# A linear-attention and feed-forward kernel on one core: the fifth token group's first dense product as seven block products, three copies of a round on ScalarE, attention steps 17 to 21 in one stretch

## The chip, the cores and the metric

The kernel runs on one core of one Trainium2 chip. The metric is the device time of the whole program in microseconds (us), lower is better. The engines are named as the profile names them: PE (TensorE, matrix multiply; PEld is its weight load), DVE (VectorE), ACT (ScalarE), POOL (GpSimd) and SP (SyncE, which issues the transfers here). Each engine works through its own list of instructions in order, and the engines wait for each other by semaphores.

## The reference

The program is a decayed linear attention followed by a feed-forward layer with a tanh GELU. Cut to what matters:

```python
# attention: q, k, v are (4, 8, 768, 64), blocks of 64 positions
for b in range(nb):
    intra = (qb @ kb^T * Dmask) @ vb
    inter = (qb * lam_pow) @ kv_state
    out[b] = intra + inter
    kv_state = lam_block * kv_state + (kb * rev_pow)^T @ vb
# feed-forward: x is (3072, 512), w_in (512, 2048), w_out (2048, 512)
h = x @ w_in                       # the first dense product
g = gelu_tanh(h)
return g @ w_out                   # the second dense product
```

## The kernel before

**Steps and token groups.** The attention is cut into 24 steps. A step is a batch's block of 256 tokens (SB) for one half of the heads, so that steps 2i and 2i+1 make token block i, of which there are 12. A step needs the loads of q, k and v (`load_step`), their scaling (`prep`: `cast_q` on DVE, `cast_k` on ACT, `scale_v` on POOL), a transposition by transfer (`transpose_dma`, issued by SP), the scores S on PE (`scores`), the causal mask on DVE that makes PT from S (`causal`), the products O = PT·v plus q·u and K = k·v on PE, the copy of O into xT on ACT (`x_out`), and the state: `update` makes t on DVE and u from t on POOL. `R(n, s)` does the scores and K of step n and the output of step s, one after the other; `burst(ns, ss)` does the same for several steps at once, with all scores first; `U(n)` is the second half of the state update of step n. The output O of a step needs u of that step and of the step two before it.

**Dense work as filler.** The 12 token blocks form seven groups, `groups` at L533: the fifth (g = 4) is blocks 6 and 7, so 512 tokens, the output of steps 12 to 15; g = 5 is steps 16 to 19, g = 6 is steps 20 to 23. As soon as a group's last x is out, `queue_group(g)` puts its dense work as small pieces into the list `filler`, and `fill(n)` runs the next n pieces. So the dense products lie on PE between the parts of the attention, in an order written by hand: the main program is a list of `burst`, `R`, `U`, `prep` and `fill` calls. `pin` keeps everything in the order of the program on each engine.

**First dense product, plain.** `mm1` (L556): for each of 16 strips of 128 columns of w_in four matmuls of 128x512 add up one PSUM bank, and one ACT instruction (L565) takes the GELU of it into gT. For a group of 512 tokens that is 64 matmuls.

**First dense product, seven block products.** Groups in `SEVEN` (L531: g = 5 and 6) use `seven(m, k)` (L726) instead. F, C and T halve w_in's columns, the contraction and the tokens. Seven products of blocks (and of sums of blocks) replace eight: `I_SUMS` are sums of blocks of w_in, made once by `sum_win`, `X_SUMS` sums of blocks of x, made for each group by `sum_x`. The work is cut into four rounds k = 0 to 3 of 256 columns of each half F. In a round each of the seven products is a piece of four matmuls of 128x256, in the order m = 1, 2, (4 of the round before), 5, 6, 3, 7. Products 1, 6, 7 and 4 add up in one bank X, of which there are two, one for even and one for odd rounds; 2 goes to a bank W; 5 and 3 add up in a bank Y. Between them the partial sums are taken out: after 1 the copy "m1" (ACT, L750), after 2 W is added to it (DVE, L760), after 5 the copy "q" (ACT), after 6 the copy "u2" (DVE, L752), after 3 Y is added to u2 (DVE), after 7 X is added to q (DVE). Because 7 adds into the same bank, it cannot start until u2 has been read out; in the same way 6 waits for the copy m1 and 3 for the copy q.

**Where the GELUs go.** The GELU of each of the four results (L756) isn't issued at once. It is put into the list `pending`, and `release()`, called right after the copy q of product 5, issues all that are pending. So in rounds 1 to 3 ACT's order is: copy q, then four GELUs (three of the round before and that of m1 of this round). In round 0 there is only one. After the last round they are issued as their sums are ready.

**Merging.** `merge` (L773) lays the pieces of `seven` between the remaining pieces of the group before (its second dense product, `product`, cut into halves of four matmuls). `SLOTS` says after which m such an old piece is put: under key 4 one old piece each after 2, 6, 3 and 7, so product 7 is the fifth piece after product 5; under key 5 there is one more after 5, so product 7 is the sixth.

**Second dense product.** `product` (L616) also uses seven block products. Its blocks of w_out and their sums are read, its own copies (L657) are on ACT.

**Order around the change before.** g = 4 is queued by `R(17, 15)`, with step 17 already under way; its first dense product is plain. Then come steps 18 and 19 in one burst, 20 and 21 in another with 32 plain matmuls of 128x512 between, and g = 5 is queued by the second with `lead` 11 and `per_set` 4.

Of the kernel before, what the change touches and what calls it, by code (L numbers as in the profile page):

```python
# [8 lines left out]
FP32 = mybir.dt.float32  # L9
FP16 = mybir.dt.float16  # L10
AF = mybir.ActivationFunctionType
ALU = mybir.AluOpType
# [3 lines left out]
def kernel(  # L16
# [10 lines left out]
    nc = tc.nc  # L27
    pin = tc.keep_in_program_order
    P = 128
    B, H, S, D = q.shape  # L30
    SB = 256
    NSB = S // SB
    HH = H // 2
    DM = H * D
    DFF = moe_w_in.shape[1]
# [9 lines left out]
    ld = ctx.enter_context(tc.tile_pool(name="ld", bufs=4))  # L45
    a16p = ctx.enter_context(tc.tile_pool(name="a16", bufs=5))
    qkp = ctx.enter_context(tc.tile_pool(name="qkp", bufs=5))
    ptp = ctx.enter_context(tc.tile_pool(name="ptp", bufs=3))
    ucp = ctx.enter_context(tc.tile_pool(name="ucp", bufs=3))
    ubp = ctx.enter_context(tc.tile_pool(name="ubp", bufs=4))  # L50
    xtp = ctx.enter_context(tc.tile_pool(name="xtp", bufs=3))
    gtp = ctx.enter_context(tc.tile_pool(name="gtp", bufs=2))
    mtp = ctx.enter_context(tc.tile_pool(name="mtp", bufs=1))
# [6 lines left out]
    def load_step(s, names="qkv"):  # L60
        b, r = divmod(s, 2 * NSB)
        sb, half = divmod(r, 2)
        ts = ld32.setdefault(s, [])
        for nm, src in (("q", q), ("k", k), ("v", v)):
            if nm not in names:
                continue
            t = ld.tile([P, HH, 2, D], FP32, tag=nm + "32", name=f"{nm}32_{s}")
            rows = src[b, half * HH : (half + 1) * HH, sb * SB : (sb + 1) * SB, :]
            queue = nc.scalar if (nm, s) == ("v", 0) else nc.sync
            pin(queue.dma_start(out=t[:].rearrange("p h j d -> p h (j d)"),  # L70
                                in_=rows.rearrange("h (p j) d -> p h (j d)", j=2)))
            ts.append(t)

    w_in16 = w16p.tile([P, NC, DFF], FP16)
    w_out16 = w16p.tile([P, NF, DM], FP16)


    HF, HE = NF // 2, DM // 2
# [65 lines left out]
    def sum_win(m, j, eng):  # L144

        if not wi_sum:
            wi_sum.extend(wst.tile([P, 2, 2, DFF // 2], FP16, tag=f"w{2 + i}", name=f"ws{i}")
                          for i in range(2))
        a, op, b = I_SUMS[m]
        cs, fs = slice(0, 2), slice(512 * j, 512 * j + 512)  # L150
        pin(eng.tensor_tensor(w_in_block(m, cs, fs), w_in_block(a, cs, fs),
                              w_in_block(b, cs, fs), op))
# [92 lines left out]
    def prep(s):  # L245
        prep_qk(s)
        prep_v(s)
# [8 lines left out]
    def prep_v(s):  # L256
        scale_v(s)
        if s >= 6:
            if s + 3 == FIRST_DMA_T + 2:
                load_step(s + 3, "qk")  # L260
            else:
                load_ahead(s + 3)
# [6 lines left out]
    def prep_qk(s):  # L269
        cast_qk(s)  # L270
        transpose_dma(s)

    def cast_qk(s):
        cast_q(s)
        cast_k(s)
# [252 lines left out]
                                for i in range(2)]  # L528
        return gs_kept[1:]

    SEVEN = (5, 6)  # L531
    SLOTS = {5: {1: 0, 2: 1, 5: 1, 6: 1, 3: 1, 7: 1}, 4: {1: 0, 2: 1, 5: 0, 6: 1, 3: 1, 7: 1}}
    groups = [[0, 1], [2], [3], [4, 5], [6, 7], [8, 9], [10, 11]]  # L533
    group_of = {sb: (g, i) for g, sbs in enumerate(groups) for i, sb in enumerate(sbs)}
# [9 lines left out]
    def queue_group(g, lead=0, per_set=0):  # L544
        N = len(groups[g]) * SB
        NTAU = N // P
        gT = gtp.tile([P, HF, 2, N], FP16, tag="gT", name=f"gT_{g}")
# [172 lines left out]
        of_set, pending = {}, []  # L720

        def release():
            while pending:
                pending.pop(0)()

        def seven(m, k):  # L726

            st = of_set.setdefault(k, {})
            for name in {1: "X", 2: "W", 5: "Y"}.get(m, ""):
                key = name + str(k % 2) if name == "X" else name  # L730
                if key not in hbank:
                    hbank[key] = ps_M.tile([P, 2, SB], FP32, tag="M", name="H" + name)
                st[name] = hbank[key]
            dst = st[{2: "W", 5: "Y", 3: "Y"}.get(m, "X")]
            a, b = X_FACTORS[m]
            for i in range(2):
                f = 2 * k + i
                for c in range(2):
                    pin(nc.tensor.matmul(  # L739
                        dst[:, i, :],  # L740
                        w_in_block(a, slice(c, c + 1), slice(f * P, f * P + P))[:, 0],
                        x_block(b, slice(c, c + 1))[:, 0],
                        start=(m in (1, 2, 5) and c == 0 and i == 0), stop=(m in (2, 3, 4) and c == 1),
                        skip_group_check=True))

            def copied(name, tag, eng):
                t = ld.tile([P, HH, 2, D], FP32, tag=tag, name=f"{name}_{g}_{k}")
                t = t[:].rearrange("p h j d -> p (h j d)").rearrange("p (i t) -> p i t", i=2)
                if eng is nc.scalar:
                    pin(nc.scalar.activation(out=t, in_=dst[:], func=AF.Copy))  # L750
                else:
                    pin(eng.tensor_copy(out=t, in_=dst[:]))  # L752
                st[name] = t

            def gelu(F, T, src):
                pin(nc.scalar.activation(out=gT[:, 2 * k : 2 * k + 2, F, T * SB : T * SB + SB],  # L756
                                         in_=src, func=AF.Gelu_apprx_tanh))

            def added(F, T, name):
                pin(nc.vector.tensor_tensor(st[name], dst[:], st[name], ALU.add))  # L760
                pending.append(lambda src=st[name]: gelu(F, T, src))

            if m == 1:
                copied("m1", "q32", nc.scalar)
            elif m == 2:
                added(0, 0, "m1")
            elif m == 5:
                copied("q", "q32", nc.scalar)
                release()
            elif m == 6:  # L770
                copied("u2", "k32", nc.vector)
            elif m == 3:
                added(0, 1, "u2")  # L773
            elif m == 7:
                added(1, 1, "q")
            elif m == 4:
                pending.insert(0, lambda: gelu(1, 0, dst[:]))
            if k == HF // 2 - 1 and m in (3, 7, 4):
                release()

# [72 lines left out]
        def behind(k, i0, i1, ms):  # L853

            piece = filler[at + k]

            def both():
                piece()
                sum_g(i0, i1, ms)

            filler[at + k] = both

        at = len(filler)
        order = [(m, p) for m in (1, 2, 5, 6, 3, 7, 4) for p in range(HN // P)]
        if g in SEVEN:
            merge(lead, per_set)
            parts = (0, 1) if g + 1 in SEVEN else (None,)
            for m, p in order:
                for part in parts:
                    filler.append(lambda m=m, p=p, part=part: product(m, p, part))  # L870
            at = len(filler) - len(order) * len(parts)
            for k, m in enumerate((2, 4, 3)):
                behind(len(parts) * k, 4, 8, (m,))
            return
        for i in range(HF):
            for fs in ([[i, i + HF]] if per == 2 else [[i], [i + HF]]):
# [1 line left out]
        for m, p in order:  # L878
            for part in (0, 1) if g + 1 in SEVEN else (None,):
                filler.append(lambda m=m, p=p, part=part: product(m, p, part))  # L880
# [9 lines left out]
        else:  # L890
            behind(9, 0, 4, (1, 2) if g == 3 else (1, 2, 4, 3))
            if g == 3:
                behind(12, 0, 4, (4, 3))
            w = 2 if g + 1 in SEVEN else 1
            for k, m in zip((0, 3, 7, 11) if w == 2 else (0, 1, 2, 4), (1, 2, 4, 3)):
                behind(n1 + k, 4, 8, (m,))

    def fill(n):
        for _ in range(min(n, len(filler))):
            filler.pop(0)()  # L900

    def R(n, s, ahead=None, keep=False):

        if n is not None:
            scores(n)
        if ahead:
            ahead()
        products(n, s)
        if n is not None:
            causal(n)  # L910
        if s is not None and s % 2 == 1:
            g, i = group_of[s // 2]
            if i == len(groups[g]) - 1 and g > 0:
                queue_group(g)
        if n is not None and not keep:
            update(n, 0)

    def U(n):
        update(n, 1)
# [138 lines left out]
            sum_win((n - 7) // 2, (n - 1) % 2, nc.vector)  # L1058

    cast_qk(16)  # L1060
    load_step(17, "qk")
    transpose_dma(16)
    load_step(17, "v")
# [13 lines left out]
    fill(1)  # L1077
    U(15)
    U(16)
    fill(8)  # L1080
    prep(18)
    R(17, 15)
    fill(1)
    U(17)
    fill(1)
    sum_win(3, 0, nc.vector)
    fill(2)
    prep(19)
    sum_win(3, 1, nc.vector)
    fill(2)  # L1090
    sum_win(4, 0, nc.vector)
    fill(2)
    sum_win(4, 1, nc.vector)
    fill(2)
    prep_qk(20)
    fill(1)
    prep_qk(21)
    prep_v(20)
    fill(3)

    burst((18, 19), (16, 17))
    prep_v(21)
    fill(2)
    U(18)
    U(19)
    fill(4)
    prep_qk(22)
    fill(2)
    burst((20, 21), (18, 19), 11, 4)
    fill(3)  # L1110
    U(20)
    U(21)
    fill(20)
    prep_qk(23)
    fill(23)
    prep_v(22)
    prep_v(23)
    fill(13)
    burst((22, 23), (20, 21))
    U(22)  # L1120
    U(23)
# [31 lines left out]
```

## Time and profile before

The time is the median of 3 runs; the profile is one execution of the program.

| | us |
|---|---|
| time, median of 3 runs | 199.15 |
| time, lowest and highest run | 198.92 and 199.36 |
| span of the profiled execution, first to last instruction | 197.1 |
| PE busy | 191.5 |
| DVE busy | 151.6 |
| ACT busy | 122.2 |
| POOL busy | 73.3 |
| from the page: share of the chain that ended last that lies on PE | 89% |

The profile names groups of instructions by line, engine, operation and tile, with the busy time of all of them, the mean duration of one and what ended the idle time before. A duration of one is longer than the distance between two of them: a matmul of 128x256 is listed with 273 ns, while 16 of them follow each other in 1.75 us in the chain. The timeline gives starts in us from the span's start, and the windows view gives for a stretch its length, the busy time of each engine, and the granted PE clock (1.00 is full).

### The profile page before, as it was taken

The page shows a single profiled execution, that of the slowest core. Times are in us where ns is not written, and L with a number is a line of the kernel's source. Part 1 is how long each engine was busy: PE and PEld are TensorE (multiplying, and loading weights), DVE is VectorE, ACT ScalarE, POOL GpSimd, SP SyncE. Part 2 cuts the span into 40 slices and gives each one's busy share as a digit, 9 for nine tenths or more (in the row PEclk, how much of TensorE's full clock was granted, in tenths as well). Part 3 has the DMA queues.
Part 4 walks back from the last instruction along what each step waited for, and adds up shares of the span by engine and source line. Part 5 has one row for each costly group of instructions (what it writes and reads, how often), then busy time and mean ns, then how long its engine had stood idle before and what let it go on. Part 6 is the DMA issues. An engine that isn't in the chain of part 4 may idle for free.

```text
span 197.1 us, 5915 instructions
## 1 busy us (share of the span) xinstructions
PE 191.5 (97%) x2431; PEld 140.0 (71%) x2431; DVE 151.6 (77%) x297; ACT 122.2 (62%) x249; POOL 73.3 (37%) x85
## 2 busy tenths in 40 slices
PE   8979999999999999999999999999999999999993
PEld 2556544446888888654688764588888888888882
DVE  4797622789999889849999937998668996588620
ACT  3673878357874685686835378844768845779221
POOL 6594123456554841068854517165002030002000
PEclk9999999999999999999999999999999999999999
DMA  6999999999999999999997998400220300030205
GB/s 172 290 324 384 387 387 388 299 287 292 236 216 225 259 343 220 213 266 247 271 268 149 268 328 213 88 4 0 53 85 25 109 6 0 0 110 0 106 19 197
DMA packets 62810, 38.13 MB, mean 193 GB/s; under 512 B 18624, under 2 KB 55744, under 8 KB 62784
## 3 DMA queue, kind: packets, MB, share of 16 engines
q1 hardware_dynamic: 62240, 37.50, 75.0%
q8 instruction: 19, 0.31, 0.6%
q10 hardware_dynamic: 544, 0.26, 0.5%
q14 instruction: 7, 0.06, 0.1%
HBM read 27.26 MB, written 6.29 MB: 170 GB/s over the span
## 4 chain that ended last, share of the span: by engine, by line
PE 89%; SPq 4%; DMA 4%; ACT 0%; issue 0%
PE Hps L561 25%; PE MX L640 18%; PE MY L640 9%; PE HX L739 7%; PE O2ps L576 7%; PE MW L640 4%; DMA wi<-in_moe_w_in_dram 4%; SPq L70 4%; PE HY L739 4%; PE S L350 3%; PE Hps L830 3%; PE HW L739 2%; PE OK L408 2%; PE O L461 1%; PE O L436 1%; PE OK L399 1%
## 5 line engine op out<-in xcount | busy, mean ns | idle before, releaser
L561 PE MATMUL Hps<-xT,w_in 128*128 128x512 f16 (+1 forms) x288 | 50.5, 332 | 0.0
L513 POOL TENSOR_TENSOR u<-t,lumask 128x256 f16<-128x256 f32 x40 | 30.9, 787 | 39.5 <-DVE t L506 25.8
L561 PEld LDWEIGHTS <-w_in 128*128 128x128 f16 x288 | 27.9, 98 | 19.1
L565 ACT ACTIVATE gT<-Hps 128x512 f16<-128x512 f32 x56 | 33.3, 597 | 11.3 <-PE Hps L561 10.8
L360 DVE TENSOR_TENSOR PT<-S,mask 128x512 f16<-128x512 f32 x48 | 30.3, 681 | 7.5 <-PE S L350 7.5
L266 POOL TENSOR_TENSOR v<-v,dv 128x512 f16<-128x512 f32 x24 | 27.7, 1156 | 18.2 <-DMA v<-in_v_dram 14.2
L640 PEld LDWEIGHTS <-gs 128*128 128x128 f16 x320 | 31.2, 98 | 3.6
L640 PEld LDWEIGHTS <-gT 128*128 128x128 f16 x240 | 23.3, 98 | 3.2 <-ACT gT L565 0.2
L640 PE MATMUL MX<-w_sum,gs 128*128 128x256 f16 x160 | 21.4, 273 | 0.0
L282 DVE TENSOR_TENSOR qk<-q,dq 128x512 f16<-128x512 f32 x23 | 18.4, 802 | 1.7 <-DMA q<-in_q_dram 1.7
L692 POOL TENSOR_TENSOR o<-u,q 128x512 f32<-128x512 f32 (+1 forms) x5 | 6.3, 1253 | 35.2 <-ACT u L657 35.2
L295 ACT ACTIVATE qk<-k 128x512 f16<-128x512 f32 x23 | 14.4, 625 | 7.4 <-DMA k<-in_k_dram 7.2
L610 DVE TENSOR_TENSOR gs<-gT 128x1024 f16<-128x1024 f16 (+1 forms) x24 | 16.9, 711 | 1.6 <-ACT gT L565 1.6
L576 PE MATMUL O2ps<-w_out,gT 128*128 128x512 f16 x64 | 14.6, 379 | 0.0
L487 ACT ACTIVATE xT<-OK 128x256 f16<-128x256 f32 x26 | 9.9, 452 | 6.7 <-PE OK L408 6.2
L739 PEld LDWEIGHTS <-ws 128*128 128x128 f16 x128 | 12.5, 97 | 1.8
L657 ACT ACTIVATE u<-MX 128x256 f32<-128x256 f32 x18 | 6.9, 384 | 10.1 <-PE MX L640 10.1
L487 ACT ACTIVATE xT<-O 128x256 f16<-128x256 f32 x22 | 8.0, 459 | 5.3 <-PE O L461 4.5
L576 PEld LDWEIGHTS <-gT 128*128 128x128 f16 x64 | 6.1, 98 | 6.6
L640 PE MATMUL MY<-w_out,gs 128*128 128x256 f16 x80 | 10.7, 273 | 0.0
L350 PEld LDWEIGHTS <-qkT 64*64 64x64 f16 x384 | 6.0, 106 | 6.6 <-issue 3.6
L640 PE MATMUL MX<-w_sum,gT 128*128 128x256 f16 x80 | 10.4, 273 | 0.0
(96 smaller groups left out, 317.3 us busy)
## 6 DMA issues: line engine op xcount, KB each, us to landing
q<-in_q_dram SPq DMA_DIRECT2D x24, 256.0 KB, 5.1
k<-in_k_dram SPq DMA_DIRECT2D x24, 256.0 KB, 5.1
v<-in_v_dram SPq DMA_DIRECT2D x23, 256.0 KB, 5.4
out_dram<-o SPq DMA_DIRECT2D x23, 256.0 KB, 4.2
wo<-in_moe_w_out_dram SPq DMA_DIRECT2D x4, 1024.0 KB, 9.5
wi<-in_moe_w_in_dram SPq DMA_DIRECT2D x4, 512.0 KB, 8.0
wi<-in_moe_w_in_dram SPq DMA_DIRECT2D x2, 1024.0 KB, 12.7
v<-in_v_dram ACTq DMA_DIRECT2D x1, 256.0 KB, 4.2
```

The lines of the kernel that those rows point to most:

```text
L266: pin(nc.gpsimd.tensor_tensor(wide(tv[:]), ld32[s][2][:], decay(dv, s), ALU.mult))
L282: pin(q_eng.tensor_tensor(wide(tq), q32[:], decay(dq, s), ALU.mult))
L295: pin(nc.scalar.activation(out=wide(tk), in_=k32[:], func=AF.Copy))
L360: pin(nc.vector.tensor_tensor(t[:, hl].rearrange("p b c d -> p b (c d)"), Sps[:].rearrange("p b c d -> p b (c d)"), mask[:].unsqueeze(1).t ...
L487: pin(nc.scalar.activation(out=d, in_=o, func=AF.Copy))
L513: pin(nc.gpsimd.tensor_tensor(u[:], state[half][:].unsqueeze(2).to_broadcast([P, 2, 2, D]), lumask[:, 2 * half : 2 * half + 2, :].unsqueez ...
L561: pin(nc.tensor.matmul(by_block(Hps[:, i, :]), w_in16[:, c, f * P : (f + 1) * P], x(c), start=(c == 0), stop=(c == NC - 1)))
L565: pin(nc.scalar.activation(out=dst, in_=Hps[:], func=AF.Gelu_apprx_tanh))
L576: pin(nc.tensor.matmul(O2[tau][0][:], gT[:, f % HF, f // HF, tau * P : (tau + 1) * P], w_out16[:, f, :], start=(n == 0), stop=(n == NF - 1)))
L610: pin(nc.vector.tensor_tensor(g_rows(m, i), g_rows(a, i), g_rows(b, i), op))
L640: pin(nc.tensor.matmul(dst, lhsT, rhs, start=(opens and i == 0), stop=(closes and i == HF - 1), skip_group_check=True))
L739: pin(nc.tensor.matmul(dst[:, i, :], w_in_block(a, slice(c, c + 1), slice(f * P, f * P + P))[:, 0], x_block(b, slice(c, c + 1))[:, 0], sta ...
```

## The change

The change does five things.

1. Group 4 joins `SEVEN`: its first dense product is made by 112 matmuls of 128x256 instead of 64 of 128x512, merged with the second product of group 3 (`lead` 7, `per_set` 5).
2. The copies m1, q and u2 of a round are all made by ACT, in groups 4, 5 and 6; u2 was on DVE.
3. m1 has a buffer of its own (`smp`, one of 2 KB per partition). q and u2 are held in parts of w_in16 and w_out16 that are no longer read (the blocks F = 1, C = 0 of w_in and rows 0 to 7 of the second half of the columns of w_out). Before, all three were in the load buffers. To make room, `ucp` (t) has 2 buffers instead of 3 and `ubp` (u) 3 instead of 4.
4. The sums of w_in for products 3 and 7 (`sum_win` 4 and 3) move: the first halves ahead of the burst of steps 13 and 14, the second halves behind `prep(19)`, inside the rounds of group 4.
5. The output of step 15 has a burst of its own, which queues group 4. All of group 4's rounds run ahead of step 17; steps 17 to 21 follow in one stretch of one burst and three `R`, with one to three pieces of filler between, and the last of them queues group 5 with `lead` 3.

```diff
-    ucp = ctx.enter_context(tc.tile_pool(name="ucp", bufs=3))
-    ubp = ctx.enter_context(tc.tile_pool(name="ubp", bufs=4))
+    ucp = ctx.enter_context(tc.tile_pool(name="ucp", bufs=2))
+    ubp = ctx.enter_context(tc.tile_pool(name="ubp", bufs=3))
+    smp = ctx.enter_context(tc.tile_pool(name="smp", bufs=1))
...
-    SEVEN = (5, 6)
+    SEVEN = (4, 5, 6)
...
+        def held(name, i):
+
+            if name == "m1":
+                t = smp.tile([P, 2, 2, P], FP32, tag="m1", name=f"m1_{g}")
+                return t[:]
+            if name == "q":
+                t = w_in16[:, 0:2, DFF // 2 + 512 * i : DFF // 2 + 512 * i + 512].bitcast(FP32)
+                return t.rearrange("p i (a t) -> p i a t", a=2)
+            t = w_out16[:, 4 * i : 4 * i + 4, HE : 2 * HE].bitcast(FP32)
+            return t.rearrange("p (i a) t -> p i a t", a=2)
...
-            def copied(name, tag, eng):
-                t = ld.tile([P, HH, 2, D], FP32, tag=tag, name=f"{name}_{g}_{k}")
...
+            def copied(name, eng):
+                st[name] = t = held(name, k % 2)
...
             elif m == 6:
-                copied("u2", "k32", nc.vector)
+                copied("u2", nc.scalar)
...
-            for k, m in enumerate((2, 4, 3)):
-                behind(len(parts) * k, 4, 8, (m,))
+            for k, m in zip((8, 10, 12) if g + 1 in SEVEN else (0, 1, 2), (2, 4, 3)):
+                behind(k, 4, 8, (m,))
...
     cast_qk(16)
+    sum_win(4, 0, nc.vector)
+    sum_win(3, 0, nc.vector)
...
     U(15)
     U(16)
+    fill(3)
+    burst((), (15,), 7, 5)
     fill(8)
     prep(18)
-    R(17, 15)
+    fill(12)
+    prep(19)
+    sum_win(4, 1, nc.vector)
+    sum_win(3, 1, nc.vector)
+    fill(12)
+    prep(20)
+    fill(14)
+    prep_qk(21)
+    fill(10)
+
+    burst((17, 18), (16,))
     fill(1)
     U(17)
+    U(18)
+    fill(2)
+    R(19, 17)
+    prep_v(21)
     fill(1)
...
+    U(19)
     fill(2)
...
+    R(20, 18)
+    fill(1)
+    U(20)
+    fill(1)
+    R(21, 19, mix=(3, 4))
     fill(2)
...
+    U(21)
+    fill(14)
     prep_qk(22)
```

More of the change, by code (lines that the diff above doesn't have):

```diff
@@ L724, in release, with quarters @@
                 pending.pop(0)()
+        def quarters(t):
+            return t.rearrange("p i (a t) -> p i a t", a=2)
[5 more added lines that the diff above has]
+                t = w_in16[:, 0:2, DFF // 2 + 512 * i : DFF // 2 + 512 * i + 512].bitcast(FP32)
+                return t.rearrange("p i (a t) -> p i a t", a=2)
+            t = w_out16[:, 4 * i : 4 * i + 4, HE : 2 * HE].bitcast(FP32)
+            return t.rearrange("p (i a) t -> p i a t", a=2)
         def seven(m, k):
@@ L744, in seven @@
                         skip_group_check=True))
-            def copied(name, tag, eng):
-                t = ld.tile([P, HH, 2, D], FP32, tag=tag, name=f"{name}_{g}_{k}")
-                t = t[:].rearrange("p h j d -> p (h j d)").rearrange("p (i t) -> p i t", i=2)
+            def copied(name, eng):
+                st[name] = t = held(name, k % 2)
                 if eng is nc.scalar:
-                    pin(nc.scalar.activation(out=t, in_=dst[:], func=AF.Copy))
+                    pin(nc.scalar.activation(out=t, in_=quarters(dst[:]), func=AF.Copy))
                 else:
-                    pin(eng.tensor_copy(out=t, in_=dst[:]))
-                st[name] = t
+                    pin(eng.tensor_copy(out=t, in_=quarters(dst[:])))
             def gelu(F, T, src):
-                pin(nc.scalar.activation(out=gT[:, 2 * k : 2 * k + 2, F, T * SB : T * SB + SB],
-                                         in_=src, func=AF.Gelu_apprx_tanh))
+                to = gT[:, 2 * k : 2 * k + 2, F, T * SB : T * SB + SB]
+                pin(nc.scalar.activation(out=quarters(to), in_=src, func=AF.Gelu_apprx_tanh))
             def added(F, T, name):
-                pin(nc.vector.tensor_tensor(st[name], dst[:], st[name], ALU.add))
+                pin(nc.vector.tensor_tensor(st[name], quarters(dst[:]), st[name], ALU.add))
                 pending.append(lambda src=st[name]: gelu(F, T, src))
             if m == 1:
-                copied("m1", "q32", nc.scalar)
+                copied("m1", nc.scalar)
             elif m == 2:
@@ L767, in seven @@
             elif m == 5:
-                copied("q", "q32", nc.scalar)
+                copied("q", nc.scalar)
                 release()
             elif m == 6:
-                copied("u2", "k32", nc.vector)
+                copied("u2", nc.scalar)
             elif m == 3:
@@ L776, in seven @@
             elif m == 4:
-                pending.insert(0, lambda: gelu(1, 0, dst[:]))
+                pending.insert(0, lambda: gelu(1, 0, quarters(dst[:])))
             if k == HF // 2 - 1 and m in (3, 7, 4):
@@ L900, in fill, with R @@
             filler.pop(0)()
-    def R(n, s, ahead=None, keep=False):
+    def R(n, s, ahead=None, keep=False, mix=()):
         if n is not None:
@@ L913, in R @@
             if i == len(groups[g]) - 1 and g > 0:
-                queue_group(g)
+                queue_group(g, *mix)
         if n is not None and not keep:
@@ L1079 @@
     U(16)
+    fill(3)
+    burst((), (15,), 7, 5)
     fill(8)
     prep(18)
-    R(17, 15)
+    fill(12)
[8 more added lines that the diff above has]
+    burst((17, 18), (16,))
     fill(1)
     U(17)
+    U(18)
+    fill(2)
+    R(19, 17)
+    prep_v(21)
     fill(1)
-    sum_win(3, 0, nc.vector)
+    U(19)
     fill(2)
-    prep(19)
-    sum_win(3, 1, nc.vector)
-    fill(2)
[L1091 to L1106, printed above, removed]
-    prep_qk(22)
[L1108 to L1113, printed above, removed]
+    R(20, 18)
[3 more added lines that the diff above has]
+    R(21, 19, mix=(3, 4))
+    fill(2)
+    U(21)
+    fill(14)
+    prep_qk(22)
+    fill(12)
     prep_qk(23)
-    fill(23)
+    fill(10)
     prep_v(22)
     prep_v(23)
-    fill(13)
+    fill(10)
     burst((22, 23), (20, 21))
```

## The prediction

> **What bounds the kernel now.** I read the page's busy times and granted clock first, then the windows from 95 us on, where the change lies, then the chain of waits there, then the timeline of one round of the seven products in group 5.
>
> ```profile
> PE 191.5 (97%) x2431; PEld 140.0 (71%) x2431; DVE 151.6 (77%) x297; ACT 122.2 (62%) x249; POOL 73.3 (37%) x85
> ...
> PEclk9999999999999999999999999999999999999999
> ```
>
> ```profile
> core 0: us, PE busy (x) PEld busy (x) DVE busy (x) ACT busy (x) POOL busy (x), PEclk, DMA share, GB/s
> 95.20:193.90 98.70, 98.62 (x1132) 79.58 (x1128) 77.17 (x133) 60.40 (x130) 25.02 (x25) 1.00 0.43 105
> ```
>
> In that window PE is busy 98.62 of 98.70 us at full clock: whatever PE no longer does there is gained, and whatever it is made to wait is lost in full. The last matmul starts near 193.8; copies and stores end the span. The span is 197.1 and the median of the runs 199.15, so 2.05 lies outside the profiled span; I sum against the span and add it.
>
> The chain gives the prices of matmuls in a dense row:
>
> ```profile
> 98.83 1.75 PE MX L640 x16
> ...
> 118.22 6.91 PE Hps L561 x32
> ```
>
> So 128x256 costs 1.75/16 = 0.1094 and 128x512 costs 6.91/32 = 0.216. A piece of four 128x256 is 0.437.
>
> **The change part by part.**
>
> *Fewer columns.* 64 x 0.216 = 13.82 goes, 112 x 0.1094 = 12.25 comes: -1.6 us. The orders of both programs on PE hold the same other matmuls, so this is the whole gain.
>
> *The copy u2 moves to ACT, behind the GELUs.* In the changed program's order on ACT, in rounds 1 to 3, stand: copy q, GELU, GELU, GELU, GELU, copy u2. Product 7 waits for u2 by an ACT semaphore; before, by one of DVE. Round 1 of group 5 before, ACT, then DVE, then PE (columns: start, duration, engine, line, what):
>
> ```profile
> 140.86 0.60 ACT L750 ACTIVATE q<-HY 128x512 f32<-128x512 f32 x1
> 141.35 0.59 ACT L756 ACTIVATE gT<-HX 128x512 f16<-128x512 f32 x1
> 141.83 0.63 ACT L756 ACTIVATE gT<-u 128x512 f16<-128x512 f32 x1
> 142.35 0.63 ACT L756 ACTIVATE gT<-q 128x512 f16<-128x512 f32 x1
> 142.87 0.63 ACT L756 ACTIVATE gT<-m 128x512 f16<-128x512 f32 x1
> 143.89 0.60 ACT L750 ACTIVATE m<-HX 128x512 f32<-128x512 f32 x1 [0.39 <-PE HX L739]
> ```
>
> ```profile
> 141.25 0.69 DVE L752 COPY u<-HX 128x512 f32<-128x512 f32 x1 [0.86 <-PE HX L739]
> ```
>
> ```profile
> 140.18 0.60 PE L739 MATMUL HY<-xs,ws 128*128 128x256 f16 x4
> 140.61 0.60 PE L739 MATMUL HX<-xs,ws 128*128 128x256 f16 x4
> ...
> 141.51 0.60 PE L739 MATMUL HY<-xT,ws 128*128 128x256 f16 x4
> ...
> 142.38 0.60 PE L739 MATMUL HX<-xs,ws 128*128 128x256 f16 x4
> ```
>
> Product 5 starts at 140.18, 6 at 140.61, 3 at 141.51, 7 at 142.38. The copy q ends at 141.46 and product 3, which waits for it, starts 0.05 later: that is the price of the hand-over. GELUs follow each other every 0.52, so after the fourth (142.87) ACT's next place is 143.39. There u2 now runs for 0.60, like m1 and q, until 143.99, and product 7 starts at 144.04 instead of 142.38: **1.66 lost**. The same reading of rounds 2 and 3 gives 147.70 + 0.52 + 0.60 + 0.05 = 148.87 against 147.20, and 153.69 against 152.03. In round 0 only one GELU lies between: 136.52 + 1.17 = 137.69 against 137.56, 0.13. Group 5: 1.66 + 1.67 + 1.66 + 0.13 = 5.1. Group 6, read in the same way (products 7 at 165.16, 169.97, 174.79, 179.62; last GELU of each round at 164.13, 170.43, 175.28, 180.11): 0.14 + 1.63 + 1.66 + 1.66 = 5.1. Nothing gives this back: PE takes products in order, the next round's product 5 is as far behind product 7 as before, and its four GELUs are again complete in their inputs when q is copied.
>
> Group 4 has one old piece more between 5 and 7, so 7 stands 6 x 0.437 = 2.62 behind 5, and the chain is 0.68 (start of 5 to start of q) + 0.49 + 0.48 + 3 x 0.52 + 0.60 + 0.05 = 3.86: 1.24 lost in a round. In rounds 1 and 3 ACT's order has a 128x256 copy of the second product between (next place 0.29 later, from 152.52 to 153.04 and such rows of L657): 1.53. Round 0 has time enough. 1.53 + 1.24 + 1.53 = 4.3.
>
> *q waits for the moved sum of w_in.* q of round 1 is written where the second half of sum 3 still reads, and ACT waits for that DVE instruction. DVE's order behind the add of round 1 is: `cast_q` 19 and two sums. I place group 4's round 1 from the unchanged PE order (step 15's output at 98.8, product 5 at 108.9): the add ends at 109.1, then 3 x 0.60 (DVE rows of this size follow each other in 0.60) puts the end at 110.9 to 111.0 instead of q's own 109.6. 1.4 more. From below 0: the 1.53 above would stay alone; from above 2.5, if cast and sums take 0.85 to 1.10 as they do beside POOL (rows of L282 and L151). I take 1.4, as POOL's v of step 19 is done by then. It isn't ACT's load: 60.40 busy of 98.70, and u2 adds 12 x 0.5 and group 4's m1, q copies 8 x 0.5.
>
> *DVE's adds of group 4* are 12 x 0.60 = 7.2 in a stretch of 21.4 on PE, with about 14 of casts, sums and group 3's adds beside; u2 of groups 5 and 6 leaves DVE. Cost nothing, hidden by PE's products, as long as product 7's add is done within the three pieces to product 4 (1.3). If that cover goes, each late add costs its lateness, at most 0.6 in four rounds; upper end 2.4.
>
> *The two early sums* run on DVE near 85.5, where the trace shows DVE idle 2.06 before the mask of steps 13 and 14 (87.53): two of 0.68 fit. Nothing. Without that room the masks of 13 and 14 would come up to 1.4 later, under 24 matmuls of 5.18.
>
> *Steps 17 to 21.* Same matmuls. R(19, 17) follows the burst after three pieces and the scores: 1.31 + 0.29. It needs u of 17, which on DVE stands behind four masks (0.60 each), then t (0.38), then u on POOL (0.67 to 1.0). DVE starts the masks late, behind the sums of gT that wait for the last GELUs, some 1.1 after the scores of 17. u comes 1.1 + 2.4 + 0.4 + 0.75 = 4.65 after those scores; PE gets there after about 0.3 + 0.7 + 1.3 + 0.3 + 0.4 + 0.4 = 3.4. **1.25 lost.** For R(20, 18) and R(21, 19) mask, t and u have been made by then; SP's transposition of step 21 now waits for the burst's last product, lands after at most 6.6 (longest of L303's transfers) and has 6.9. From 0 (DVE on time) to 3.5 (each of the three R late by about 1.2). ACT's stores, POOL's v of 21 and the loads are hidden by the same row of matmuls. Fewer t and u buffers add waits for long finished readers: nothing.
>
> *Sum:* -1.6 + 4.3 + 1.4 + 5.1 + 5.1 + 1.25 = +15.6. Span 197.1 + 15.6 = 212.7, median **214.7**.
>
> **Two rules of the Trainium skill.** The row: one PSUM read of 512 columns is 0.60 on ACT and 0.69 on DVE, and before both share them. "TensorEngine Tiling (Array Packing)", section "PSUM Bottleneck", advises to spread reads of PSUM over ScalarE and VectorE. That speaks against the third copy on ACT; with u2 left on VectorE the sum would be without the 14.2 of rounds 1 to 3 and near 200.5. The row for the clock is 1.00 in every window. "TensorE: Matmul & The Clock Gate", section "HAM oscillation", warns of PE gaps over some 3.4 us; the longest here is 2.9 by my sum, so by the page the clock stays, and no row here shows it otherwise.
>
> **Rivals.**
> *The wait isn't on the path (faster).* If product 7 finds u2 read in time, because ACT's GELUs stand elsewhere or the pieces between cover 3.9 us, only -1.6 and the stretch remain: 197.5 to 198.8. It decides from the point where all stalls together are under 1.6, so 0.18 a round in nine rounds. For it: ACT has 38% free. Against: the order on ACT and the semaphore, and a round's place 143.39 is read, not guessed. 5%.
> *DVE and ACT jam further (slower still).* The strided copies and adds into the weights could cost more. Six ACT instructions a round, each 0.10 longer, cost 9 x 0.6 = 5.4; with the upper ends of the sums and the R (1.1 + 2.3) the median is 223. For it: no row shows this shape; against: xT and k casts with four-part shapes (0.38, 0.62) cost what plain ones do. 12%.
> *Half the loss.* If in groups 5 and 6 rounds lose only a part (GELUs at 0.48, a shorter copy), say 1.2 instead of 1.66 in six rounds, and R and the q wait cost nothing: 214.7 - 2.8 - 2.65 = 209.3. 13%.
>
> **Numbers.** Forecast 214.7 with 70%, own range 211 to 218. To leave out no more than two in ten I take 208.5 to 220. A change within 0.2% can't be told from none here. Faster comes from the first rival alone: 0.04; same 0.01; slower 0.95.
>
> **What would show it.** Right: in the timeline after, product 7 of rounds 1 to 3 starts 0.05 behind the end of u2, and u2 behind four GELUs; PE idle in 95 to 210 of some 17 us, most of it before HX and put down to ACT; one gap of near 3 in group 4's round 1. Wrong: PE busy near 98% again, or gaps put down to DVE's adds, or a clock under 1.00.

## The result, and the profile after

| | before | after |
|---|---|---|
| median, us | 199.1 (198.92 to 199.36, 4 runs) | 223.1 (222.08 to 225.6, 4 runs) |
| ratio to before, 95% interval | | 1.119, 1.1162 to 1.1218 |
| profiled span, us | 197.1 | 221.5 |
| outside the span (median minus span), us | 2.0 | 1.6 |

The change makes the kernel 24 us slower. The forecast was 214.7 with a range up to 220.0: the direction was right, and the time lies 3.1 us above the range. One of the four runs after, the one of 225.6, was a slow one, and the ratio leaves it out. Run by run the time lies 1.7 to 1.9 above the span, before and after alike: the 2.0 and 1.6 of the table set a median against one profile, and the prediction's 2.05 was some 0.25 too much. What has to be explained is 24.4 us of span, where the prediction had 15.6.

The page of the changed kernel (busy time and share of the span for each engine; then the granted PE clock in 40 slices):

```profile
PE 195.9 (88%) x2477; PEld 144.4 (65%) x2479; DVE 153.1 (69%) x305; ACT 132.4 (60%) x269; POOL 71.3 (32%) x85
...
PEclk9999999999999999999997999999999999999999
```

PE was busy 97% of the span and is now busy 88%. No other engine comes near a full share, so none has become the bound as a whole. One slice of the clock row has a 7. The windows view places the loss. From step 15's output to the last matmul (before: 98.62 of 98.70 us busy):

```profile
core 0: us, PE busy (x) PEld busy (x) DVE busy (x) ACT busy (x) POOL busy (x), PEclk, DMA share, GB/s
95.20:217.90 122.70, 103.56 (x1183) 84.39 (x1182) 77.12 (x140) 70.61 (x149) 22.42 (x26) 0.99 0.35 86
```

PE is idle for 19.1 us here. Its busy time rises by 4.9 as well, although it now has fewer columns to do. Two things add to it: a fall of the clock, further down, adds 1.4, and a matmul ahead of a wait is listed 0.16 longer than its place in a dense row. They don't make up the whole 4.9. The waits view says whom PE waits for (engine, line, who releases it: us in all, times, longest):

```profile
PE HX L754 <- ACT w_out L764: 14.4, 10, 1.8
...
PEld L754 <- DVE w_in L773: 4.4, 9, 0.6
...
ACT w_in L764 <- DVE ws L152: 2.1, 1, 2.1
...
PE HX L754 <- DVE w_in L773: 2.0, 8, 0.3
```

L754 is now the matmul of `seven`, L764 its copies, L770 its GELUs, L773 its adds, L152 `sum_win`. `w_out` is the place of u2, `w_in` the place of q. So product 7 waits ten times for the copy u2, as forecast. The nine waits of a weight load (PEld) for a DVE add into the place of q were not forecast; eight of them hold up a matmul on PE. Both can be seen in round 1 of group 5. PE first (start, duration, what; in brackets the idle time before and its releaser):

```profile
149.78 0.60 PE L641 MATMUL MX<-w_sum,gs 128*128 128x256 f16 x4
150.21 0.27 PE L754 MATMUL HX<-xT,w_in 128*128 128x256 f16 x1
150.81 0.50 PE L754 MATMUL HX<-xT,w_in 128*128 128x256 f16 x3 [0.33 <-DVE w_in L773]
...
154.21 0.60 PE L641 MATMUL MY<-w_out,gs 128*128 128x256 f16 x4
156.28 0.60 PE L754 MATMUL HX<-xs,ws 128*128 128x256 f16 x4 [1.47 <-ACT w_out L764]
```

ACT in the same round:

```profile
153.10 0.60 ACT L764 ACTIVATE w_in<-HY 128x512 f32<-128x512 f32 x1
153.59 0.59 ACT L770 ACTIVATE gT<-HX 128x512 f16<-128x512 f32 x1
154.07 0.63 ACT L770 ACTIVATE gT<-w_out 128x512 f16<-128x512 f32 x1
154.59 0.63 ACT L770 ACTIVATE gT<-w_in 128x512 f16<-128x512 f32 x1
155.11 0.63 ACT L770 ACTIVATE gT<-m 128x512 f16<-128x512 f32 x1
155.63 0.60 ACT L764 ACTIVATE w_out<-HX 128x512 f32<-128x512 f32 x1
```

Copy q, four GELUs, copy u2: u2 ends at 156.23, and product 7 starts at 156.28, just the 0.05 that the prediction read off the old round. The old piece before it starts at 154.21 and takes 0.437, so PE would have been ready at 154.65: 1.63 lost. (The row says 1.47, because a matmul's listed duration overlaps the start of the next. I take the distance between starts, less what the work between takes in a dense row.)

The second loss is the line at 150.81. Product 1 of round 2 begins at 150.21 with one matmul. The next should start at 150.32 and starts at 150.81: 0.49. Nothing of the values needs this wait. q is held in columns 1024 to 2047 of rows C = 0 and 1 of w_in16, and product 1 reads as weights the first half of the columns of these rows. Its matmul for row 0 goes ahead, that for row 1 waits.

Summed over PE's timeline in this way:

| where | predicted | measured |
|---|---|---|
| fewer columns | -1.6 | -1.6 (not measured by itself) |
| product 7 behind u2, 12 rounds | 14.5 | 16.7, with 0.45 of the wait for the sum below |
| matmul of product 1 behind the add into q, 8 times 0.40 to 0.49 | not seen | 3.3 |
| q of group 4's round 1 behind the moved sum | 1.4 | 1.07 at product 3, and 0.45 more at product 7 |
| granted clock after that gap | none | 1.4 |
| group 5 round 0: product 5 behind the sums of x | none | 0.9 |
| steps 17 to 21 | 1.25 | about 1.5 |
| sum | 15.6 | 23.3 of 24.4 |

Of the rest 0.3 lies ahead of 95.5 us and 0.25 behind the last matmul; the other 0.5 is not assigned.

### The profile page after: what moved, and what is told of

Its sections match the earlier page's. It is cut to its first block, busy times and chain, and to the rows that moved or that the text cites. A ratio compares the mean times of both kernels' runs of the same rounds, so it can differ in the third digit from the quotient of the medians.

```text
span 221.5 us, 6038 instructions
## 1 busy us (share of the span) xinstructions
PE 195.9 (88%) x2477; PEld 144.4 (65%) x2479; DVE 153.1 (69%) x305; ACT 132.4 (60%) x269; POOL 71.3 (32%) x85
## 5 line engine op out<-in xcount | busy, mean ns | idle before, releaser
L562 PE MATMUL Hps<-xT,w_in 128*128 128x256 f16 (+1 forms) x224 | 36.2, 318 | 0.0
L754 PEld LDWEIGHTS <-ws 128*128 128x128 f16 x192 | 18.6, 98 | 21.4 <-issue 17.9
L562 PEld LDWEIGHTS <-w_in 128*128 128x128 f16 x224 | 21.8, 98 | 12.3
L566 ACT ACTIVATE gT<-Hps 128x512 f16<-128x512 f32 x40 | 23.7, 596 | 8.6 <-PE Hps L562 8.3
L754 PE MATMUL HX<-xs,ws 128*128 128x256 f16 x96 | 14.8, 277 | 14.9 <-ACT w_out L764 14.4
L773 DVE TENSOR_TENSOR w_out<-HY,w_out 128x512 f32<-128x512 f32 x12 | 8.3, 691 | 27.2 <-ACT w_out L764 27.2
L641 PEld LDWEIGHTS <-gT 128*128 128x128 f16 x240 | 23.1, 98 | 3.0 <-issue 0.3
L754 PEld LDWEIGHTS <-w_in 128*128 128x128 f16 x144 | 13.7, 100 | 6.4 <-DVE w_in L773 4.4
L764 ACT ACTIVATE m<-HX 128x512 f32<-128x512 f32 x12 | 7.2, 597 | 17.5 <-PE HX L754 17.5
L488 ACT ACTIVATE xT<-OK 128x256 f16<-128x256 f32 x30 | 11.6, 454 | 7.8 <-PE OK L409 5.0
L773 DVE TENSOR_TENSOR m<-HW,m 128x512 f32<-128x512 f32 x12 | 8.3, 689 | 7.5 <-ACT m L764 7.5
```

The lines of the kernel that those rows point to most:

```text
L562: pin(nc.tensor.matmul(by_block(Hps[:, i, :]), w_in16[:, c, f * P : (f + 1) * P], x(c), start=(c == 0), stop=(c == NC - 1)))
L566: pin(nc.scalar.activation(out=dst, in_=Hps[:], func=AF.Gelu_apprx_tanh))
L641: pin(nc.tensor.matmul(dst, lhsT, rhs, start=(opens and i == 0), stop=(closes and i == HF - 1), skip_group_check=True))
L754: pin(nc.tensor.matmul(dst[:, i, :], w_in_block(a, slice(c, c + 1), slice(f * P, f * P + P))[:, 0], x_block(b, slice(c, c + 1))[:, 0], sta ...
L764: pin(nc.scalar.activation(out=t, in_=quarters(dst[:]), func=AF.Copy))
L773: pin(nc.vector.tensor_tensor(st[name], quarters(dst[:]), st[name], ALU.add))
```

## The experiments

All kernels compute the whole reference. Lines of code are of the changed kernel, if nothing else is said. "Back" is the median of after, 223.1, less that of the experiment.

| | median, us | range | ratio to before, 95% interval | span |
|---|---|---|---|---|
| e1_u2_vector | 208.91 | 208.84 to 209.35 | 1.0482, 1.0421 to 1.0544 | 207.1 |
| e2_gelus_behind_u2 | 208.42 | 207.97 to 209.88 | 1.0466, 1.0393 to 1.0538 | 206.2 |
| e3_before_u2_scalar | 208.84 | 208.77 to 211.21 | 1.0511, 1.0415 to 1.0608 | 207.1 |
| e8_before_gelus_behind_u2 | 199.38 | 199.26 to 199.57 | 1.0015, 1.0005 to 1.0025 | 197.6 |
| e4_sum_early | 223.09 | 222.02 to 224.56 | 1.1194, 1.1107 to 1.1281 | 222.2 |
| e7_sums_only | 222.48 | 221.67 to 223.27 | 1.119, 1.1144 to 1.1236 | 220.0 |
| e5_no_weight_waits | 218.04 | 217.85 to 218.3 | 1.0956, 1.0936 to 1.0976 | 216.0 |
| e6_all_undone | 204.06 | 203.9 to 204.09 | 1.0251, 1.0234 to 1.0268 | 202.3 |
| e9_later_start | 203.69 | 203.35 to 204.75 | 1.0241, 1.0217 to 1.0265 | 202.2 |
| e10_later_start_5 | 203.67 | 203.26 to 204.3 | 1.0243, 1.0225 to 1.026 | 201.5 |

The mean granted clock isn't the same in all runs of a kernel, and it moves the time. After took 222.08 at 0.998, and 222.95 and 223.26 at 0.992. e2 took 207.97 and 208.09 near 1.00, 208.75 and 209.88 at 0.989; e4 222.02 and 222.20 at 1.00, 223.99 and 224.56 near 0.99; e7 221.67 and 221.76 near 1.00, 223.21 and 223.27 near 0.99. All runs of e5 and e6 have 0.998 or more. So some 1 us of a number "back" can be the clock, and a smaller difference is read at like clock.

### Is it the place of u2 in ACT's order? (e1, e2, e3, e8)

e1 gives u2 back to DVE and changes nothing else:

```diff
             elif m == 6:
-                copied("u2", nc.scalar)
+                copied("u2", nc.vector)
```

> The changed kernel with one word undone: the copy u2 back on DVE, all else as changed. Theory (u2 behind the GELUs on ACT is the main loss): its trace shows product 7 late by 0.63, 1.93, 1.19, 1.47 in group 4, 1.64 and three times 1.63 in group 5, 0.14 and three times 1.63 in group 6, 16.7 in all; these go, and the 1.4 of the lower clock with them if the long gap is their doing: 205.0 to 206.5. Rival (DVE is the bound, and u2 was moved to relieve it): DVE takes 12 copies of 0.60 more and is late instead; over 212.

208.91: 14.2 back, or 13.2 from after's 222.08 at a like clock. e2 leaves u2 on ACT and lets the GELUs go behind it:

```diff
             elif m == 5:
                 copied("q", nc.scalar)
-                release()
             elif m == 6:
                 copied("u2", nc.scalar)
+                release()
```

> The changed kernel with u2 on ACT, but the pending GELUs released behind the copy u2 instead of behind the copy q. Theory: the order on ACT is the loss, not its load; u2 then ends before product 7's place, the same 16.7 to 18.1 go: 205.0 to 206.5, like the run with u2 on DVE or up to 0.5 below it. Rival (ACT has too much work with three copies a round): the GELUs are late for the next round's copies and most of the loss stays, over 214.

208.42: 14.7 back. In both, the rows "PE HX L754 <- ACT w_out L764" are gone. Both come out some 2 us above the range expected. In part another wait grew in the room made: the same weight load in group 5's first rounds, behind DVE. e2's rows of that wait on PE, first the whole, then the longest one:

```profile
PE HX L754 <- DVE w_in L773: 4.1, 9, 2.0
```

```profile
145.01 0.50 PE L754 MATMUL HX<-xT,w_in 128*128 128x256 f16 x3 [1.97 <-DVE w_in L773]
```

It was 2.0 in all after, at most 0.33 each. In e1 product 7 also waits twice for the copy on DVE, 1.7 in all. So undoing one cause gives back less than it cost, since PE then reaches the next wait earlier.

e3 and e8 take the same two orders to the kernel before, which has none of the rest of the change. e3:

```diff
             elif m == 6:
-                copied("u2", "k32", nc.vector)
+                copied("u2", "k32", nc.scalar)
```

> The kernel before with u2 on ACT and nothing else changed. Theory: 5.1 in group 5 and 5.1 in group 6, as worked out in the prediction: 209.3. Rival (the loss needs the new places of q and u2 in the weights, or the moved steps): under 202.

e8 in addition has the `release()` of the copy q behind that copy of u2.

> The kernel before with u2 on ACT and the GELUs released behind it. Theory: the ten us of the run with u2 on ACT come from the order on ACT alone; u2 then ends at product 5's start + 1.9, product 7 stands at + 2.2: 199.1, within 0.4. Rival (ACT's load with three copies and four GELUs a round): 202 or more.

e3: 208.84, 9.9 above before's 198.97 of the same session, with six waits in groups 5 and 6 that are all alike; two of them:

```profile
144.17 0.60 PE L739 MATMUL HX<-xs,ws 128*128 128x256 f16 x4 [1.47 <-ACT u L750]
150.60 0.60 PE L739 MATMUL HX<-xs,ws 128*128 128x256 f16 x4 [1.47 <-ACT u L750]
```

Six times 1.63 is 9.8. e8: 199.38, 0.3 us above before by the ratio, with the same copies on the same engine. Its ACT in the same round, then its PE:

```profile
140.96 0.60 ACT L750 ACTIVATE q<-HY 128x512 f32<-128x512 f32 x1
141.45 0.59 ACT L750 ACTIVATE u<-HX 128x512 f32<-128x512 f32 x1
141.93 0.60 ACT L756 ACTIVATE gT<-HX 128x512 f16<-128x512 f32 x1
```

```profile
142.04 0.60 PE L640 MATMUL MY<-w_out,gs 128*128 128x256 f16 x4
142.48 0.60 PE L739 MATMUL HX<-xs,ws 128*128 128x256 f16 x4
```

u2 ends at 142.04, product 7 starts at 142.48 without a wait. This settles two things. The loss comes from the order on ACT alone, and the rest of the change isn't needed for it. And it is not ACT's load: with three copies of a round on ACT and the GELUs behind them the kernel loses 0.15%.

The prediction weighed against this copy what the Trainium skill says on "TensorEngine Tiling (Array Packing)", section "PSUM Bottleneck": to use both ScalarE and VectorE for the reads of PSUM. With u2 on VectorE (e1) 14.2 us return, so its advice agrees in sign. But e8, with all three copies on ScalarE, shows that here the order counts for 9.9 us and the split for about 0.3.

### Is it the moved sum, and what does it cost? (e4, e7)

e4 puts the two second halves of the sums far ahead of group 4:

```diff
     burst((13, 14), (12,))
     fill(1)
     U(13)
     U(14)
+    sum_win(4, 1, nc.vector)
+    sum_win(3, 1, nc.vector)
...
     prep(19)
-    sum_win(4, 1, nc.vector)
-    sum_win(3, 1, nc.vector)
```

> The changed kernel with the second halves of the sums of w_in for products 4 and 3 moved ahead of group 4's rounds, behind the state update of steps 13 and 14. Theory: the copy q of group 4's round 1 no longer waits for them: product 3's wait of 1.07 and 0.45 of product 7's go, and the 1.4 of the lower clock if that gap brings it on: 220.0 to 221.5. Rival (DVE is too full ahead of the rounds): the gain is given back in front, 222.5 to 224.

223.09, no gain: the theory's number missed. The wait for the sum is gone, but DVE has no room there either, and the masks of the burst behind it come late. PE of e4, and its granted clock in windows:

```profile
97.41 0.81 PE L562 MATMUL Hps<-xT,w_in 128*128 128x512 f16 x3 [2.05 <-DVE PT L361]
```

```profile
98.00:100.00 2.00, 2.00 (x7) 0.78 (x6) 2.00 (x7) 0.61 (x2) 0.39 (x1) 0.62 0.79 154
100.00:102.00 2.00, 2.00 (x6) 0.72 (x5) 2.00 (x4) 0.89 (x2) 1.24 (x2) 0.52 0.99 286
```

PE waits 2.05 for the masks, and behind that gap the clock falls (0.62, then 0.52), as it does after the gap in after. The two runs in which the clock stayed at 1.00 (222.02 and 222.20) are no faster than after's one at 0.998 (222.08) either. Nothing is settled on the sum's price by e4, but it shows that this place would have been no better.

e7 makes both sums of product 4 on DVE where the change had one of each, and those of product 3 on POOL, earlier:

```diff
         if n == 12:
+            sum_win(3, 0, nc.gpsimd)
+            sum_win(3, 1, nc.gpsimd)
...
     sum_win(4, 0, nc.vector)
-    sum_win(3, 0, nc.vector)
+    sum_win(4, 1, nc.vector)
...
     prep(19)
-    sum_win(4, 1, nc.vector)
-    sum_win(3, 1, nc.vector)
```

> The changed kernel with only the four sums moved ahead (4 on DVE, 3 on POOL), q where the change puts it. Theory: product 3's wait 1.07 and 0.45 of product 7's go and the clock stays up in group 4's round 1 (1.4): 220.0 to 220.5, and the difference to the run with q in one row is the weight waits, 3.6. Rival (the moved sums delay masks or v and cost in front what they save, as on DVE): 222.5 or more.

222.48, with an interval that overlaps after's: it can't be told from no gain. The wait of q is gone. The fall of the clock is gone from the profiled run (mean clock 0.999, after 0.992), but two of the other three runs have 0.991 and 0.992 and took 223.2 and 223.3, so taking away this wait didn't keep the clock up in every run; where it fell in those two isn't known. At like clock e7 is 0.3 to 0.4 below after's 222.08. POOL takes 4.21 us for two sums and so makes u late:

```profile
87.89 4.21 POOL L152 TENSOR_TENSOR ws<-w_in 128x1024 f16<-128x1024 f16 x2
```

```profile
96.08 0.40 PE L462 MATMUL O<-qkT,u 128*128 128x128 f16 x4 [0.71 <-POOL u L514]
96.65 0.28 PE L462 MATMUL O<-qkT,u 128*128 128x128 f16 x2 [0.17 <-POOL u L514]
```

So the sum's own price can be read from after's timeline, but no run gained it.

### The weight loads that wait for the add into q (e5)

e5 is e7, with each q laid in one row of w_in16 and no longer across two. An even round has it in row C = 0, an odd one in row C = 1:

```diff
             if name == "q":
-                t = w_in16[:, 0:2, DFF // 2 + 512 * i : DFF // 2 + 512 * i + 512].bitcast(FP32)
-                return t.rearrange("p i (a t) -> p i a t", a=2)
+                t = w_in16[:, i, DFF // 2 : DFF].bitcast(FP32)
+                return t.rearrange("p (i a t) -> p i a t", i=2, a=2)
```

It needs e7's early sums, since a whole row is now written in round 0.

> The changed kernel; u2 stays behind the GELUs, but q is held in one row of w_in's unread block (row k mod 2, 1024 wide) instead of half of both rows, so that the weight loads of product 1 of the next round no longer wait for the DVE add into q, and all four sums of w_in for products 4 and 3 are made ahead of group 4 (4 on DVE, 3 on POOL while it waits for the loads of v), so that q waits for none. Theory: nine weight waits of 0.40 (3.6), product 3's 1.07 with 0.45 of product 7's, and the 1.4 of the lower clock go: 223.1 - 6.5 = 216.5. Rival (the weight loads wait in the shadow of the copy u2, so nothing on the path): 221 or more.

218.04, against e7's 222.48: 4.4 less. Part of that is the clock: against e7's two runs near 1.00 it is 3.7. The rows "PEld L754 <- DVE w_in L773" and "PE HX L754 <- DVE w_in L773" are no longer in the waits of e5. Same sizes, same engines, same instructions: only the address of q differs. That a write to two rows is held to cover what lies between them, the first half of row 1 among it, fits all of this (row 0's weight isn't held up, row 1's is, and a q within one row holds up none); I have not seen it in the program itself. In e7's timeline nine matmuls of product 1 wait 0.40 to 0.49, 3.7 in all: just what comes back.

### All three undone (e6), and what is left (e9, e10)

e6 is e5 with the `release()` of e2.

> The run with the GELUs behind u2, with q in one row and the sums ahead as in the run before it. Theory: 208.4 less the weight waits (eight of 0.40 and one of 2.1, of which some 0.4 to 1.5 is DVE being late anyway) less 1.06 of product 3: 202.0 to 203.5. What is left above 197.5 is then the stretch of steps 17 to 21 and DVE's lateness behind it. Rival (the weight waits aren't real stalls): 207 or more.

204.06, so 14.0 less than e5, and 4.4 less than e2 (4.0 at like clock), which has the waits of weight loads and the old sums. The two causes add up with little overlap. In group 4's four rounds PE has no wait of 0.1 us or more. What is left over before, 5.2 us of span, lies around them; all of e6's waits on PE that the timeline names from 86 us to 150 us:

```profile
95.98 0.40 PE L462 MATMUL O<-qkT,u 128*128 128x128 f16 x4 [0.71 <-POOL u L514]
96.56 0.29 PE L462 MATMUL O<-qkT,u 128*128 128x128 f16 x2 [0.17 <-POOL u L514]
126.68 0.32 PE L451 MATMUL K<-v,qk 64*64 64x64 f16 x9 [0.38 <-ACT o L658]
127.17 0.32 PE L451 MATMUL K<-v,qk 64*64 64x64 f16 x15 [0.17 <-ACT gT L770]
130.69 0.28 PE L409 MATMUL OK<-qkT,u 128*128 128x128 f16 x2 [0.41 <-POOL u L514]
138.54 0.61 PE L754 MATMUL HY<-xs,ws 128*128 128x256 f16 x4 [0.74 <-DVE xs L719]
143.94 0.60 PE L754 MATMUL HX<-xs,w_in 128*128 128x256 f16 x4 [1.21 <-DVE w_in L773]
```

3.8 us of rows, so with the 1.6 that fewer columns should have gained not all of the loss is named; the first two belong to e7's sums on POOL, the other five to the stretch of steps 17 to 21 and the start of group 5 behind it. The last two are DVE's: in 126 to 146 it is busy 18.22 of 20.00 us.

My theory was that these two are a backlog, which a later start of group 5 would let DVE work off. e9 gives it four old pieces more; e10, with (5, 4) in the same place, gives it two:

```diff
-    R(21, 19, mix=(3, 4))
+    R(21, 19, mix=(7, 4))
```

> As e6_all_undone (204.06), but group 5's first round begins seven old pieces after it is queued and not three; all matmuls are the same. Theory (what is left behind steps 17 to 21 is DVE's backlog of masks, t and sums of x, seen in e6 as the waits 0.74 before product 5 and 1.21 between rounds 0 and 1, and four pieces of 0.44 give DVE 1.75 to work it off): both waits go, 201.9 to 202.8. Rival (the backlog is only met later, by the GELUs or the sums of gT at the end of the group): 203.6 or more.

> As e9_later_start, with a lead of five old pieces, so 0.87 more room than e6 has. Theory: the wait of 0.74 goes and 0.1 to 0.9 of the 1.21 stays: 202.3 to 203.4, between e6 and e9_later_start. Rival: within 0.4 of e6's 204.06.

203.69 and 203.67: 0.4 below e6, with intervals that overlap its own. The theory fell and the rival holds. In e9 both waits are gone, and three others stand in their place. One is for a sum of gT at 138.40 (0.42), one for the copy q at 156.28 (0.25), and the longest comes at the end of the group:

```profile
158.33 0.60 PE L754 MATMUL HX<-xs,w_in 128*128 128x256 f16 x4 [0.96 <-DVE w_in L773]
```

This is product 4 of the last round. It waits for the add behind product 7, and no old piece lies between them any more: those used for the later start are missing here. No version beat the kernel before. The best with the seven products in group 4 are e9 and e10, at 1.024 of before; they can't be told apart.

## Why the prediction was wrong in size

- **u2 behind the GELUs: right, in mechanism and size.** Predicted 1.66 a round in rounds 1 to 3 of groups 5 and 6, measured 1.63; in group 4's rounds 2 and 3 predicted 1.24 and 1.53, measured 1.19 and 1.47. Round 0 of group 6 gives 0.14, as forecast. Shown by e1, e2, e3 and e8.
- **The step that failed first: q and u2 in the weights.** The prediction asked who waits for the copies and adds, but priced their new places only for the sum that still read them. It took "strided copies" for the risk, and these cost nothing (the copies of L764 are listed with 597 ns, the adds of L773 with 689 to 691, as the 0.60 and 0.69 of before). It did not ask who else reads rows that the new place touches. The answer was product 1's weight load: eight times 0.40 to 0.49 on PE, 3.3 us by the timeline of after, and 3.7 us by e5 against e7 at like clock. It is the largest missing term, though the next is close.
- **The second: "DVE's adds of group 4 cost nothing", with DVE on time.** In round 0 of groups 4 and 5 one GELU stands before u2, and it waits for the add of m1, which is late on DVE. ACT of after, group 4 and group 5:

```profile
106.06 0.63 ACT L770 ACTIVATE gT<-m 128x512 f16<-128x512 f32 x1 [0.85 <-DVE m L773]
106.60 0.58 ACT L764 ACTIVATE w_out<-HX 128x512 f32<-128x512 f32 x1
```

```profile
148.18 0.63 ACT L770 ACTIVATE gT<-m 128x512 f16<-128x512 f32 x1 [1.52 <-DVE m L773]
148.71 0.58 ACT L764 ACTIVATE w_out<-HX 128x512 f32<-128x512 f32 x1
```

  So a late DVE reaches PE through ACT's order: 0.63 lost where 0 was forecast, and 1.64 where 0.13 was. In e2, where u2 stands ahead of that GELU, product 7 waits in neither round. In group 5 product 5 also waits 0.9 for the sums of x. Together 3.0. The cover of "three pieces" that I named was that of the last add, and the place to look was the first.
- **The third: the clock "stays".** I had one gap of near 3 us in group 4's round 1. There are two gaps, with two pieces between them, and behind them the clock fell. PE of after, and windows of 2 us there:

```profile
113.08 0.60 PE L754 MATMUL HY<-xT,ws 128*128 128x256 f16 x4 [0.91 <-ACT w_in L764]
113.51 0.60 PE L641 MATMUL MX<-w_sum,gs 128*128 128x256 f16 x4
115.88 1.01 PE L754 MATMUL HX<-xs,ws 128*128 128x256 f16 x4 [1.77 <-ACT w_out L764]
116.69 1.06 PE L641 MATMUL MY<-w_out,gs 128*128 128x256 f16 x4
...
119.01 0.60 PE L754 MATMUL HX<-xs,w_in 128*128 128x256 f16 x4
```

```profile
114.00:116.00 2.00, 0.23 (x2) 0.10 (x1) 0.14 (x1) 2.00 (x6) 0.00 (x0) 0.84 0.92 265
116.00:118.00 2.00, 2.00 (x11) 1.29 (x10) 1.24 (x2) 0.10 (x1) 0.00 (x0) 0.50 0.41 118
118.00:120.00 2.00, 2.00 (x17) 1.63 (x16) 0.68 (x2) 1.12 (x2) 0.00 (x0) 0.81 0.00 0
```

  From 115.88 to 119.01 four pieces take 3.13 and not 1.75: 1.4 lost. This isn't in every run of the kernel: the one with a mean clock of 0.998 took 222.08.
- **q behind the sum:** predicted 1.4, measured 1.07 at product 3 and about 0.45 more at product 7, so nearly right as a reading of the timeline. What the gap did to the clock was missing, and no experiment got the time back (e4, e7).
- **Steps 17 to 21:** 1.25 predicted, some 1.5 measured; u of 17 from POOL, the wait that was forecast, is only one of the waits, 0.41 by the row; another is 0.20 for a mask. So here the number was nearer than the mechanism. e6, e9 and e10 show that the stretch and group 5's start keep several us even with all else undone; how much of that is the new order, and how much is DVE work that group 4 has left behind, was not told apart.
- **The rivals:** "not on the path" and "half the loss" are out. "DVE and ACT jam further" gave 223 (its terms add up to 223.5), the time that came, but its price was made of longer instructions, which no row shows. It hit the number by luck, with another mechanism. Of the signs of being wrong two came beside the signs of being right: waits put down to DVE's adds, and a clock under 1.00.

## What to carry to other kernels

On an engine that works in order, price a moved instruction by what stands ahead of it there and not by the engine's busy share: the same copy, in eight rounds, cost 9.9 us behind the GELUs and 0.3 us ahead of them. When data is put into a spare part of a tile that others still read, look at every reader of the rows it touches, and keep it within one row where possible (3.7 us here). A stall that is taken away pays only up to the next wait behind it (e4, e7, e9), so follow the timeline one round further before a gain is counted.

## What the runs showed of the hardware that was not expected

- **The clock fell after shorter gaps than I had allowed for.** In the profile of after, PE was idle for about 1.0 us, busy for 0.87, idle for 1.9, and the granted clock then was 0.50 over 2 us. In e4 one wait of 2.05 behind a stretch of small matmuls was followed by 0.62 and 0.52. The waits of 1.47 in after and e3, each some 5 us of work apart, left it at 1.00, and so did e2's one of 1.97. The Trainium skill, "TensorE: Matmul & The Clock Gate", section "HAM oscillation", warns of idle gaps above some 3.4 us; here the measurement decides, and less was enough. The gaps alone don't settle it: of the four runs of after, e4 and e7 each, some kept a mean clock of 0.998 to 1.00 and some had 0.990 to 0.992, and of 13 runs of the kernel before one had 0.991. What exactly is summed, these runs don't tell.
- **Sums on POOL are slow.** A 128x1024 f16 sum takes 2.1 us there (4.21 for two), and 0.7 to 1.5 on DVE (in after 0.68 at 111.65, 1.50 at 148.06).
